# Opening of a fused attention and gated MLP block: left-over weight rows on ScalarE's queue and in pieces, column sums 32 wide, keys ahead, V of chunk 1 behind the transposes of chunk 2

## Chip, cores and metric

The kernel runs on one core of one Trainium2 chip. The metric is the device time of one execution in microseconds (us), lower is better. An engine is named as in the profile: PE is TensorE, DVE is VectorE, ACT is ScalarE, POOL is GpSimd, and SP is SyncE, which in this kernel only issues DMAs.

## The reference, cut to what matters

All inputs are bfloat16. S = 2048 tokens, D = 576, H = 32 heads of 18, F = 4608.

```python
mod = (silu(c) @ w_mod).reshape(1, 6, 1, 576)          # c is 1 x 576, w_mod is 576 x 3456
sa, ca, ga, sb, cb, gb = mod[:, 0], ..., mod[:, 5]
h = layernorm(x) * (1 + ca) + sa
x = x + ga * attention(h, wqkv, wo)                    # each token sees 8 keys: itself and 2, 4, ... 14 before it
h = layernorm(x) * (1 + cb) + sb
x = x + gb * (((h @ w_gate) * (h @ w_up)) @ w_down)
```

The reference's attention gathers eight keys and values for each token (missing ones at the start are masked), takes the softmax over the eight logits of each head, sums the values, and multiplies with wo.

## The kernel before

**Tiles.** The tokens are cut into eight chunks of 256 (CH), each of two tiles of 128 (ST). D = 576 is four full blocks of 128 rows and one left-over block of 64 rows. So every weight with 576 input rows has five k-tiles (KT), the last of which (kt = KF = 4) fills 64 partitions only; its other 64 partitions are set to zero.

**Order.** The schedule is manual: every engine runs its instructions in the order in which the program emits them. The order in the opening is written out by hand, as calls that interleave three chunks. Waits for data, and for buffers, are semaphores set by the tile framework from what is read and written. The DMAs that SP and ACT issue share eight semaphore slots, taken in turn in program order, and an issue waits for the landing of the DMA that held its slot before.

**Opening loads.** SP loads, in this order: x of chunk 0 in two tiles, the five k-tiles of wmA (the columns sa and ca of w_mod, order MODK), wqk (the query and key columns of wqkv, order QKK) with x of chunk 1 before the fourth, wv, x of chunk 2, wmB (sb, cb), wo in four pieces, wmC (ga), later tokens, wgr, and five blocks of gate and up weights (load_wgu). wgr holds the 64 left-over rows of w_gate and w_up, one above the other on 128 partitions, for all 4608 columns. ACT loads only c.

**Modulation columns.** `sc` is silu(c) as a column for each k-tile. `pm_part(kt)` multiplies the wmA blocks with it, ten matmuls for each kt, each of one output column; `pm` is the sum over kt. `run_idle(n)` puts n matmuls on zeros between. `t0(j)` transposes the normalised tile j of chunk 0, and `mod0` evicts it with the modulation into hT0. `qk0(j, kt)` accumulates queries and keys of tile j over k-tiles as they land; the calls go (0,0) (0,1) (1,0) (0,2) (1,1) (0,3) (1,2) (0,4) (1,3) (1,4), where the second number counts along QKK.

**Chunk 0's attention** is done without a gather: `pj` multiplies queries with shifted keys, `lj` sums them into logits, `max_j` and `sum_j` do the softmax, whose result is `attn`. `to_keys(j)` shifts `attn` from queries to keys by matmuls with a shifted identity (`slide`) into `pk`, and ACT copies that to `keyed`. `av_mul(j, hf)` multiplies the values with `keyed` on DVE, and `av_sum(j, hf)` sums the products, shifted, on TensorE into `po`.

**Chunks 1 and 2 beside it.** `a_t(i, ...)` transposes the normalised chunk i, tile by tile, and evicts five tiles of hT (three on DVE, two on ACT); `between` is called after the first token tile's transposes. hT comes from a pool with one buffer (`hTp`), so that chunk 2's hT lies where chunk 1's lay. `a_v(i, j)` computes the values of one token tile from hT and wv (matmuls `pv` and `pvr`), ACT copies them to `v_sb`, and a DMA on POOL's queue stores them. `a_q(i, g)` computes group g of queries and keys. `mod_columns` and `mod_row` make the other modulation values; the row of ga is two matmul groups, `pa` of 512 columns and `pb` of 64. `b_wj` ends chunk 0's attention with wo, `norm2` and `transposed` prepare h2T, and the matmuls of gate and up (L645) then run over groups of token tiles to the end of the kernel.

The part of the order that the change moves:

```python
    for j in range(ST):
        a_v(1, j)
    ga_out = []
    a_t(2, (0, 1, 2), lambda: ga_out.append(mod_row(..., ga_bc, sc_bc)))
    for j in range(ST):
        to_keys(j)
    ga_out[0]()
    av_mul(0, 0)
    av_mul(0, 1)
    a_q(2, 0)
    av_sum(0, 0)
```

Of the kernel before, what the change touches and what calls it, by code (L numbers as in the profile page):

```python
# [7 lines left out]
BF = mybir.dt.bfloat16  # L8
F32 = mybir.dt.float32
ALU = mybir.AluOpType  # L10
# [6 lines left out]
SYNC = mybir.DependencyInfo(mybir.DependencyClass.Sync, mybir.DependencyReason.DATA)  # L17

P = 128
D = 576  # L20
DP = 640
KT = 5
KF = 4
# [4 lines left out]
FF = 4608  # L28
# [5 lines left out]
ST = CH // P  # L34
# [2 lines left out]
VA = 28  # L37
VR = H - VA

MODK = (0, 1, 4, 2, 3)  # L40
QKK = (0, 1, 4, 2, 3)
GROUPS = [(0, 2), (2, 6), (6, 10), (10, 13), (13, 16)]

# [2 lines left out]
def kernel(  # L46
# [13 lines left out]
    nc = tc.nc  # L60
# [30 lines left out]
    def ps(shape, dt, name):  # L91
        return psp.tile(shape, dt, name=name, tag="bank")
# [4 lines left out]
    def col(m):  # L97
        return js(m) if m < KF else slice(D - P, D)
# [3 lines left out]
    addc = consts.tile([P, 2, KT], F32, name="addc")  # L102
    eps = consts.tile([P, 1], F32, name="eps")
    modc = consts.tile([P, 4, KT], F32, name="modc")
# [39 lines left out]
    def load_wgu(g):  # L144
        if g >= NG * NBLK:
            return
        cs = slice((g % NBLK) * NB, (g % NBLK + 1) * NB)
        wb = (wgx if g in (3, 4, NBLK - 1) else wgup).tile([P, KF, 2, NB], BF, name="wgu")
        for t, wsrc in enumerate((B_w_gate, B_w_up)):
            r = nc.sync.dma_start(wb[:, :, t, :], wsrc[0:KF * P, cs].rearrange("(k p) n -> p k n", p=P))  # L150
        wgu_blk[g] = wb
        wgu_in[g] = r

    def load_wgr():
        for t, wsrc in enumerate((B_w_gate, B_w_up)):
            r = nc.sync.dma_start(wgr[64 * t:64 * (t + 1), :], wsrc[KF * P:D, :])
        return r

    def load_wd(g):
        if g >= NG * NBLK:  # L160
# [6 lines left out]
    def load_k(dst, wsrc, c0, n):  # L167
        r = nc.sync.dma_start(dst(slice(0, P), slice(0, KF)), wsrc[0:KF * P, c0:c0 + n].rearrange("(k p) n -> p k n", p=P))
        nc.sync.dma_start(dst(slice(0, 64), KF), wsrc[KF * P:D, c0:c0 + n])
        return r  # L170

    def load_wm2(wm, blk):
        for p, k in ((slice(0, P), slice(0, KF)), (slice(0, 64), KF)):
# [10 lines left out]
    def run_idle(n):  # L184
        idle = ps([P, P], F32, "idle")
        for _ in range(n):
            nc.tensor.matmul(idle[:], lhsT=zero[:], rhs=zero[:], start=True, stop=True, skip_group_check=True)
# [5 lines left out]
    nc.vector.memset(addc[:, 1, :], 1.0)  # L193
    nc.scalar.dma_start(c_row[0:KF, :], c[0, 0:KF * P].rearrange("(m p) -> m p", p=P))
    nc.scalar.dma_start(c_row[KF:KT, 0:D - KF * P], c[0:1, KF * P:D])
    nc.scalar.preload_act_table_set("natural_log_exp_and_others")
    nc.gpsimd.memset(ident[:], 0.0)
    nc.gpsimd.affine_select(out=ident[:], in_=ident[:], compare_op=ALU.not_equal, fill=1.0, base=0,
                            pattern=[[-1, P]], channel_multiplier=1)
# [1 line left out]
    wmC = wdp.tile([P, FB, D], BF, name="wd")  # L201
    wmCr = x1p.tile([P, D], BF, name="x1")
    nc.gpsimd.memset(wmA[64:, KF, :, :], 0.0)
    nc.gpsimd.memset(wmCr[64:, :], 0.0)
    halves = lambda t: t.rearrange("p (b n) -> p b n", b=2)

    def rows(kt):
        return slice(0, P if kt < KF else 64), slice(kt * P, min(D, (kt + 1) * P))

    for kt in MODK:  # L210
        p, r = rows(kt)
        nc.sync.dma_start(wmA[p, kt, :, :].rearrange("p b n -> p (b n)"), w_mod[r, 0:2 * D])
    for kt in QKK:
        if kt == QKK[3]:
            load_x(1)
        p, r = rows(kt)
        nc.sync.dma_start(wqk[p, kt, :], A_wqkv[r, 0:2 * D])
    load_k(lambda p, k: wv[p, k, :], A_wqkv, 2 * D, D)


# [86 lines left out]
    def mod_row(wm, dst, sc_bc, parts=((0, 512), (512, D))):  # L307
        outs = []
        for c0, c1 in parts:
            p_t = ps([P, c1 - c0], F32, "pa" if c0 == 0 else "pb")  # L310
            for kt in range(KT):
                nc.tensor.matmul(p_t[:], lhsT=sc_bc[:, kt, :], rhs=wm(slice(0, P), kt)[:, c0:c1],
                                 start=(kt == 0), stop=(kt == KT - 1))
            outs.append((dst[:, c0:c1], p_t))

        def evict():
            for d, p_t in outs:
                nc.scalar.copy(d, p_t[:])
        return evict
# [15 lines left out]
    def a_tiles(i):  # L335
        hT = hTp.tile([P, KT, CH], BF, name="hT") if i else vshp.tile([P, KT, CH], BF, name="vsh")
        aa[i].update(hT=hT, qT=qTs[i % 2], kT=kTs[i % 2])
# [8 lines left out]
    def a_t(i, on_dve=(0, 1, 2), between=None):  # L346
        a_tiles(i)
        hT = aa[i]["hT"]
        transposed(aa[i]["xn"], lambda m: hT[:, m, :], (0, 1), 0, between)(on_dve)
# [25 lines left out]
    def a_q(i, g):  # L375
        qk_tiles(i, QGRP[g], slice(0, CH), nc.scalar.copy)
        if g == 2:
            a_halo(i)
# [4 lines left out]
    def a_v(i, j):  # L383
        hT = aa[i]["hT"]
        pv = ps([P, VA * DH], F32, "pv")
        pvr = ps([P, VR * DH], F32, "pvr")
        for kt in range(KT):
            nc.tensor.matmul(pv[:], lhsT=hT[:, kt, js(j)], rhs=wv[:, kt, 0:VA * DH], start=(kt == 0), stop=(kt == KT - 1))  # L388
        for kt in range(KT):
            nc.tensor.matmul(pvr[:], lhsT=hT[:, kt, js(j)], rhs=wv[:, kt, VA * DH:D], start=(kt == 0), stop=(kt == KT - 1))  # L390
        v_sb = vstage.tile([P, DH, H], BF, name="v_sb")[:] if i else v0(j)
        nc.scalar.copy(v_sb[:, :, 0:VA], pv[:].rearrange("p (h d) -> p d h", d=DH))
        nc.scalar.copy(v_sb[:, :, VA:H], pvr[:].rearrange("p (h d) -> p d h", d=DH))
        r0 = HALO + i * CH + j * P
        if i == 0:
            if j == 1:
                nc.gpsimd.dma_start(vd[r0 + P - HALO:r0 + P, :], o_sbs[0][P - HALO:P, j, 0:D])
            return
        nc.gpsimd.dma_start(vd[r0:r0 + P, :], v_sb.rearrange("p d h -> p (d h)"))
# [99 lines left out]
    def to_keys(j):  # L499
        pk = ps([P, W, H], F32, "pk")  # L500
        for w in range(W):
            sh = DIL * (W - 1 - w)
            at = attn0[:, w // 4, :, w % 4, :]
            cross = j == 0 and sh > 0
            nc.tensor.matmul(pk[:, w, :], lhsT=slide[:, P + sh:2 * P + sh], rhs=at[:, j, :], start=True, stop=not cross,
                             skip_group_check=True)
            if cross:
                nc.tensor.matmul(pk[:, w, :], lhsT=slide[:, sh:P + sh], rhs=at[:, 1, :], start=False, stop=True,
                                 skip_group_check=True)
        kt = lgp.tile([P, W, H], BF, name="keyed", tag="lgs")  # L510
        nc.scalar.copy(kt[:], pk[:])
        keyed.append(kt)
# [266 lines left out]
    c_col = ps([P, KT], F32, "c_col")  # L779
    nc.tensor.matmul(c_col[:], lhsT=c_row[:], rhs=ident[0:KT, 0:KT], start=True, stop=True)  # L780
    e_f = sp.tile([P, KT], F32, name="e_f")
    nc.scalar.activation(e_f[:], c_col[:], ACTF.Exp, scale=-1.0)
    stat0(0)
    rsq0(slice(0, 1))
    nc.vector.tensor_scalar_add(e_f[:], e_f[:], 1.0)
    nc.vector.reciprocal(e_f[:], e_f[:])
    nc.vector.tensor_tensor(sc[:], c_col[:], e_f[:], ALU.mult)
    stat0(1)
    rsq0(slice(1, 2))
    for j in range(ST):  # L790
        norm0(j)
    a_tiles(0)
    a_halo(0)
    nc.vector.memset(wo[64:, KF, :], 0.0)
# [6 lines left out]
    for kt in QKK:  # L801
        nc.gpsimd.tensor_copy(halves(wq4[:, kt, :]), halves(wqk[:, kt, :])[:, :, KF * P:D])

    pm = ps([P, 2, KT], F32, "pm")
    trA, trB = ps([P, 3, CH], BF, "tr_pA"), ps([P, 2, CH], BF, "tr_pB")
    tr = [trA[:, m, :] if m < 3 else trB[:, m - 3, :] for m in range(KT)]

    def pm_part(kt):
        for bi in range(2):
            for m in range(KT):  # L810
                nc.tensor.matmul(pm[:, bi, m:m + 1], lhsT=wmA[:, kt, bi, col(m)], rhs=sc[:, kt:kt + 1],
                                 start=(kt == MODK[0] and bi == 0 and m == 0), stop=(kt == MODK[-1]), skip_group_check=True)

    def t0(j):
        for m in range(KT):
            nc.tensor.transpose(tr[m][:, js(j)], xn0[:, j, js(m)], ident[:])

    run_idle(10)
    pm_part(MODK[0])
    run_idle(6)  # L820
    pm_part(MODK[1])
    t0(0)
    run_idle(4)
    t0(1)
    pm_part(MODK[2])
    run_idle(4)
    pm_part(MODK[3])
    run_idle(8)
    pm_part(MODK[4])
# [2 lines left out]
    def mod0(j, m, on_dve):  # L832
        modulate(hT0[:, m, js(j)], tr[m][:, js(j)], m, 1, 0, on_dve)

    nc.vector.tensor_tensor(modc[:, 0:2, 0:KF], pm[:, :, 0:KF], addc[:, :, 0:KF], ALU.add)
    mod0(0, 0, True)
    nc.vector.tensor_tensor(modc[0:64, 0:2, KF:KT], pm[64:P, :, KF:KT], addc[64:P, :, KF:KT], ALU.add)
    for j in range(ST):
        for m in (1, 2) if j == 0 else (0, 1, 2):
            mod0(j, m, True)  # L840
# [63 lines left out]
        nc.vector.tensor_tensor(attn0[:, :, j], dd0[:, j].rearrange("p (a w) h -> p a w h", a=2),  # L904
                                ss[:, None, None, :].to_broadcast([P, 2, 4, H]), ALU.mult)

    def behind(dma, load):
        tc.add_manual_dep(dma.ins, load.ins.name, SYNC, reason="value rows go first")

    load_x(2)  # L910
    wmB = sp.tile([P, KT, 2, D], BF, name="wmB", tag="wm")
    nc.gpsimd.memset(wmB[64:, KF, :, :], 0.0)
# [5 lines left out]
    load_k(lambda p, k: wmCr[p, :] if k == KF else wmC[p, k, :], w_mod, 2 * D, D)  # L918
    load_res(0)
    load_x(3)  # L920
    load_wgr()
    for g in range(5):
        load_wgu(g)

    for w in range(3):
# [38 lines left out]
    aa[2]["norm"]((0,))  # L964
    sum_j(1)
    aa[2]["norm"]((1,))
    for j in range(ST):
        a_v(1, j)
    ga_out = []
    a_t(2, (0, 1, 2), lambda: ga_out.append(mod_row(lambda p, k: wmC[p, k, :] if k < KF else wmCr[p, :], ga_bc, sc_bc)))  # L970
    for j in range(ST):
        to_keys(j)
    ga_out[0]()
    av_mul(0, 0)
    av_mul(0, 1)
    a_q(2, 0)
    av_sum(0, 0)
    av_mul(1, 0)
    av_sum(0, 1)
# [43 lines left out]
    first = []  # L1023
# [56 lines left out]
```

## Time and profile before

| quantity | value |
|---|---|
| median of 3 runs | 561.76 us (560.91 to 562.95) |
| profiled execution | 562.59 us |
| its span, first to last instruction | 560.9 us |
| busy PE / DVE / ACT / POOL | 550.2 / 330.7 / 248.5 / 67.1 us |
| moved by DMA | 108.14 MB, mean 193 GB/s |
| first matmuls of the opening | 1.06 us |
| first query and key matmul of chunk 0 | 11.78 us |
| first matmul of gate and up | 51.76 us |

The profiled execution is longer than its span by 1.69 us, which lie ahead of the first and behind the last instruction. "Busy" counts every recorded instruction, the matmuls on zeros too. In the timelines that follow a row is a group of like instructions on one engine: start and length in us, engine, line, operation, output and inputs, shape, count, and in brackets the idle time just before it with the engine or DMA that released it. Ends of matmuls are modelled, so that rows of PE can overlap. In the table by windows each engine's column is its busy time with the number of instructions in brackets, and the last three are the granted TensorE clock, the busy share of the DMA engines and what they moved.

### The profile page before, as it was taken

How to read it: one execution, taken by the hardware profiler on the slowest of the kernel's cores; microseconds unless marked ns; L12 is line 12 of the kernel's file. 1: busy time of each engine (PE TensorE's matmuls, PEld its weight loads, DVE VectorE, ACT ScalarE, POOL GpSimd, SP SyncE). 2: the span in 40 equal slices, each digit the busy share in tenths (PEclk: the TensorE clock that was granted, in tenths of full speed). 3: DMA queues.
4: the chain of work that ended last, by engine and by line, in shares of the span. 5: the costliest groups of instructions: out<-in, count | busy, mean ns of one | idle time of the engine just before them, and what ended most of it. 6: DMA issues, size and time to landing. Idle time of an engine off the chain costs nothing.

```text
span 560.9 us, 14310 instructions
## 1 busy us (share of the span) xinstructions
PE 550.2 (98%) x6019; PEld 329.5 (59%) x6057; DVE 330.7 (59%) x798; ACT 248.5 (44%) x572; POOL 67.1 (12%) x104
## 2 busy tenths in 40 slices
PE   8999999999999999999999999999999999999996
PEld 7878886665444446666444445655556555556564
DVE  6888898985677777251858686406736614322202
ACT  2645566344555662323355654230466511455500
POOL 5102201223000001111100100121100022000020
PEclk9999999999999999999999999999999999999999
DMA  8999999745646745232834856334966565565063
GB/s 252 279 270 307 341 295 352 238 131 172 239 153 200 241 149 177 70 125 96 292 122 151 266 174 190 85 106 128 326 184 196 182 196 174 183 191 187 1 172 115
DMA packets 69514, 108.14 MB, mean 193 GB/s; under 512 B 3562, under 2 KB 57658, under 8 KB 69322
## 3 DMA queue, kind: packets, MB, share of 16 engines
q1 hardware_dynamic: 58272, 61.42, 35.9%
q0 software_dynamic: 11168, 45.81, 25.6%
q8 instruction: 47, 0.77, 0.6%
q14 instruction: 17, 0.14, 0.1%
q10 hardware_dynamic: 10, 0.00, 0.0%
HBM read 102.78 MB, written 4.44 MB: 191 GB/s over the span
## 4 chain that ended last, share of the span: by engine, by line
PE 56%; issue 29%; POOL 3%; DMA 1%; DVE 1%; ACT 1%; POOLq 0%; ACTq 0%
PE pg L645 17%; PE pu L645 14%; PE acc L712 11%; PE pq L365 4%; POOL wd L165 2%; PE accr L716 2%; PE pw L562 2%; PE pv L388 2%; PE lg L423 1%; DMA wd<-in_B_w_down_dram 1%; PE tr_pA L287 1%; PE tr_pB L287 0%; PE oT_pA L493 0%; DVE o_t L751 0%; PE pwr L560 0%
## 5 line engine op out<-in xcount | busy, mean ns | idle before, releaser
L645 PE MATMUL pg<-h2T,wgu 64*128 64x512 bf16 (+2 forms) x1440 | 277.3, 334 | 0.0
L645 PE MATMUL pu<-h2T,wgu 64*128 64x512 bf16 (+2 forms) x1440 | 276.0, 334 | 0.0
L645 PEld LDWEIGHTS <-wgu 64*128 64x128 bf16 x2880 | 141.6, 94 | 106.9 <-issue 0.5
L669 ACT CAST u_sb<-pu 128x512 bf16<-128x512 f32 (+2 forms) x180 | 90.2, 501 | 136.1 <-PE pg L645 134.5
L712 PE MATMUL acc<-wd,hh 128*128 128x512 bf16 (+1 forms) x556 | 140.4, 370 | 0.4
L674 DVE TENSOR_TENSOR hh<-g_sb,u_sb 128x512 bf16<-128x512 bf16 (+2 forms) x180 | 66.7, 372 | 99.2 <-ACT g_sb L670 97.7
L716 PE MATMUL accr<-wd,hh 128*128 128x64 bf16 x576 | 99.4, 193 | 1.8 <-DMA wd<-in_B_w_down_dram 0.2
L670 ACT CAST g_sb<-pg 128x512 bf16<-128x512 f32 (+2 forms) x180 | 91.3, 507 | 0.0
L712 PEld LDWEIGHTS <-hh 128*128 128x128 bf16 x588 | 55.2, 98 | 57.8 <-issue 1.7
L165 POOL DMA_DIRECT2D wd<-in_B_w_down_dram x45 | 33.8, 751 | 292.3 <-PE accr L716 237.8
L645 PE MATMUL pu<-h2T,wgr 64*128 64x512 bf16 (+2 forms) x180 | 60.3, 335 | 0.3 <-ACT u_sb L669 0.3
L645 PE MATMUL pg<-h2T,wgr 64*128 64x512 bf16 (+2 forms) x180 | 60.3, 335 | 0.2 <-DVE h2T L274 0.2
L716 PEld LDWEIGHTS <-hh 128*128 128x128 bf16 x576 | 51.9, 98 | 3.2 <-issue 0.7
L413 DVE TENSOR_TENSOR prod<-qT,kT 128x1280 bf16<-128x1280 bf16 x56 | 44.8, 818 | 2.6 <-PE lg L423 2.6
L473 DVE TENSOR_TENSOR vsh<-vsh,attn 128x1152 bf16<-128x1152 bf16 x56 | 41.0, 751 | 0.0
L365 PE MATMUL pq<-hT,wqk 128*128 128x256 bf16 x280 | 35.3, 273 | 0.1
L274 DVE TENSOR_SCALAR h2T<-tr_pA,modc 128x256 bf16<-128x256 bf16 (+1 forms) x27 | 8.8, 382 | 36.9 <-PE tr_pA L287 36.9
L365 PEld LDWEIGHTS <-wqk 128*128 128x128 bf16 x280 | 25.6, 98 | 5.2 <-issue 0.4
L645 PEld LDWEIGHTS <-wgr 64*128 64x128 bf16 x360 | 18.0, 94 | 17.0 <-issue 4.5
L407 POOL DMA_DIRECT2D vsh<-vd x14 | 12.4, 890 | 123.3 <-DVE o_sb L484 84.4
L368 ACT CAST qT<-pq 128x512 bf16<-128x512 f32 x14 | 8.2, 582 | 27.8 <-PE pq L365 27.8
L480 DVE TENSOR_TENSOR vsh<-vsh 128x1152 bf16<-128x1152 bf16 x28 | 20.5, 752 | 0.0
(186 smaller groups left out, 485.5 us busy)
## 6 DMA issues: line engine op xcount, KB each, us to landing
wd<-in_B_w_down_dram POOLq DMA_DIRECT2D x45, 576.0 KB, 4.5
wgu<-in_B_w_gate_dram SPq DMA_DIRECT2D x45, 512.0 KB, 4.4
wgu<-in_B_w_up_dram SPq DMA_DIRECT2D x45, 512.0 KB, 5.6
vsh<-vd POOLq DMA_DIRECT2D x14, 1152.0 KB, 8.0
x_r<-in_A_x_dram SPq DMA_DIRECT2D x8, 288.0 KB, 7.4
out_dram<-x SPq DMA_DIRECT2D x15, 144.0 KB, 6.8
x_t<-in_A_x_dram SPq DMA_DIRECT2D x7, 288.0 KB, 5.7
vd<-v_sb POOLq DMA_DIRECT2D x14, 144.0 KB, 4.1
```

The costliest lines, as they stand in the source:

```text
L165: return nc.gpsimd.dma_start(wb[:], B_w_down[r0:r0 + FB * P, :].rearrange("(k p) n -> p k n", p=P))
L365: nc.tensor.matmul(pq[:, gi, :], lhsT=qk_w(kt, m), rhs=hT[:, kt, cols], start=(kt == 0), stop=(kt == KT - 1))
L407: return nc.gpsimd.dma_start(vsh[:].rearrange("p w d h -> p w (d h)"), vsrc)
L413: nc.vector.tensor_tensor(prod[:], aa[i]["qT"][:], aa[i]["kT"][:, :, off:off + CH], ALU.mult)
L473: nc.vector.tensor_tensor(v, v, at, ALU.mult)
L480: nc.vector.tensor_tensor(vsh[:, d], vsh[:, d], vsh[:, 4 + 2 * s:6 + 2 * s], ALU.add)
L645: return nc.tensor.matmul(bank[:, 0:N], lhsT=lhs, rhs=rhs, start=first, stop=last, skip_group_check=True)
L669: nc.scalar.copy(u[:, 0:N], pu[:, 0:N])
L670: nc.scalar.copy(g[:, 0:N], pg[:, 0:N])
L674: nc.vector.tensor_tensor(hh[:, f, 0:N], gu[0][:, 0:N], gu[1][:, 0:N], ALU.mult)
L712: nc.tensor.matmul(a[:], lhsT=hh[:, f, js(j)], rhs=wb[:, f % FB, cs], start=(f == 0), stop=(f == FT - 1))
L716: nc.tensor.matmul(accr[:, j, :], lhsT=hh[:, f, js(j)], rhs=wb[:, f % FB, 512:D], start=(f == 0 and j == 0), stop=(f == FT - 1), skip_grou ...
```

## The change

The left-over 64 rows (kt = 4) of wmA and of wqk are now loaded by ACT's queue: wmA's directly behind c, ahead of the load of the activation table, and wqk's after the second `rsq0`, with a dependency (`behind`) on the landing of wmA's k-tile 2. SP loads the full k-tiles 0 to 3 of both. MODK becomes (0, 4, 1, 2, 3). wgr is loaded in four quarters of its columns, each before the wgu block of the same number, eight DMAs in place of two.

`sc` is computed 32 columns wide (`sc_w`), and the matmuls of `pm_part` have 32 equal columns, of which the first is read. `sc` itself is copied from it behind the norms. The matmuls on zeros are put at other places: 20, 4, 2, 8 and 5 in place of 10, 6, 4, 4, 8 and 5 after the first 24.

Behind the softmax the order becomes: a_v(1,0), the ga row's first 512 columns, the transposes of chunk 2's first tile, the ga row's last 64 columns, `to_keys` of both tiles, the transposes of the second tile, a_v(1,1), then av_mul and a_q(2,0), and only then the evictions of the ga row.

```diff
-MODK = (0, 1, 4, 2, 3)
+MODK = (0, 4, 1, 2, 3)
...
-    def load_wgr():
+    def load_wgr(q):
+        cs = slice(q * FF // 4, (q + 1) * FF // 4)
         for t, wsrc in enumerate((B_w_gate, B_w_up)):
-            r = nc.sync.dma_start(wgr[64 * t:64 * (t + 1), :], wsrc[KF * P:D, :])
-        return r
+            nc.sync.dma_start(wgr[64 * t:64 * (t + 1), cs], wsrc[KF * P:D, cs])
...
-    nc.scalar.preload_act_table_set("natural_log_exp_and_others")
...
+    nc.scalar.dma_start(wmA[0:64, KF, :, :].rearrange("p b n -> p (b n)"), w_mod[KF * P:D, 0:2 * D])
+    nc.scalar.preload_act_table_set("natural_log_exp_and_others")
...
-    for kt in MODK:
+    def load_wmA(eng, kt):
         p, r = rows(kt)
-        nc.sync.dma_start(wmA[p, kt, :, :].rearrange("p b n -> p (b n)"), w_mod[r, 0:2 * D])
-    for kt in QKK:
-        if kt == QKK[3]:
+        return eng.dma_start(wmA[p, kt, :, :].rearrange("p b n -> p (b n)"), w_mod[r, 0:2 * D])
+
+    def load_qk(eng, kt):
+        p, r = rows(kt)
+        return eng.dma_start(wqk[p, kt, :], A_wqkv[r, 0:2 * D])
+
+    wmA_in = [load_wmA(nc.sync, kt) for kt in range(KF)]
+    for kt in range(KF):
+        if kt == 2:
             load_x(1)
-        p, r = rows(kt)
-        nc.sync.dma_start(wqk[p, kt, :], A_wqkv[r, 0:2 * D])
+        load_qk(nc.sync, kt)
...
-    nc.vector.tensor_tensor(sc[:], c_col[:], e_f[:], ALU.mult)
+    wide = lambda t: t[:, :, None].to_broadcast([P, KT, 32])
+    nc.vector.tensor_tensor(sc_w[:], wide(c_col), wide(e_f), ALU.mult)
     stat0(1)
     rsq0(slice(1, 2))
+    behind(load_qk(nc.scalar, KF), wmA_in[2])
     for j in range(ST):
         norm0(j)
+    nc.vector.tensor_copy(sc[:], sc_w[:, :, 0])
...
-    pm = ps([P, 2, KT], F32, "pm")
+    pm = ps([P, 2, KT, 32], F32, "pm")
...
-                nc.tensor.matmul(pm[:, bi, m:m + 1], lhsT=wmA[:, kt, bi, col(m)], rhs=sc[:, kt:kt + 1],
+                nc.tensor.matmul(pm[:, bi, m, :], lhsT=wmA[:, kt, bi, col(m)], rhs=sc_w[:, kt, :],
...
-    run_idle(10)
+    run_idle(20)
     pm_part(MODK[0])
-    run_idle(6)
     pm_part(MODK[1])
     t0(0)
     run_idle(4)
+    pm_part(MODK[2])
     t0(1)
-    pm_part(MODK[2])
-    run_idle(4)
+    run_idle(2)
     pm_part(MODK[3])
     run_idle(8)
     pm_part(MODK[4])
...
-    load_wgr()
     for g in range(5):
+        if g < 4:
+            load_wgr(g)
         load_wgu(g)
...
-    for j in range(ST):
-        a_v(1, j)
-    ga_out = []
-    a_t(2, (0, 1, 2), lambda: ga_out.append(mod_row(lambda p, k: wmC[p, k, :] if k < KF else wmCr[p, :], ga_bc, sc_bc)))
-    for j in range(ST):
-        to_keys(j)
-    ga_out[0]()
+    a_v(1, 0)
+    ga_row = lambda part: mod_row(lambda p, k: wmC[p, k, :] if k < KF else wmCr[p, :], ga_bc, sc_bc, (part,))
+    ga_out = [ga_row((0, 512))]
+
+    def between():
+        ga_out.append(ga_row((512, D)))
+        for j in range(ST):
+            to_keys(j)
+
+    a_t(2, (0, 1, 2), between)
+    a_v(1, 1)
     av_mul(0, 0)
     av_mul(0, 1)
     a_q(2, 0)
+    for out in ga_out:
+        out()
     av_sum(0, 0)
```

The reads of `pm` take column 0 of the 32, and `behind` moves to an earlier place in the file with its text unchanged.

## The prediction

> **What bounds the kernel now.** I read the page first, sections 1 and 4, then TensorE's waits, then stage windows and timelines of the opening, the only stage the diff reaches.
>
> ```profile
> PE 550.2 (98%) x6019; PEld 329.5 (59%) x6057; DVE 330.7 (59%) x798; ACT 248.5 (44%) x572; POOL 67.1 (12%) x104
> ```
>
> TensorE is busy for 550.2 of 560.9 us. The matmuls of gate_up begin at 51.76 (first h2T wait) and are dense from there, so what the opening gains or loses before 51.76 I pass on to the end one for one. The waits of TensorE up to 60 us say how little there is:
>
> ```profile
> PE idle L187 <- DVE c_row L190: 1.1, 1, 1.1
> PE pm L811 <- DMA wmA<-in_w_mod_dram: 0.9, 2, 0.6
> PE po L531 <- DVE vsh L520: 0.7, 1, 0.7
> PE lgj L888 <- DVE prodj L880: 0.3, 1, 0.3
> ```
>
> But "busy" counts idle matmuls (L187) that only keep the array warm; in the first 17 us they hide waits for loads. The windows show that stage (engine columns: busy, count; last three: clock, DMA share, GB/s):
>
> ```profile
> 3.50:7.00 3.50, 2.69 (x30) 1.94 (x28) 3.27 (x10) 1.07 (x5) 3.23 (x10) 1.00 0.92 257
> 7.00:10.40 3.40, 3.35 (x55) 3.35 (x56) 1.85 (x9) 0.07 (x1) 1.46 (x4) 1.00 1.03 336
> 10.40:13.20 2.80, 2.63 (x33) 2.39 (x32) 2.01 (x9) 1.25 (x4) 0.88 (x3) 1.00 1.07 307
> 13.20:17.00 3.80, 3.80 (x69) 3.69 (x67) 2.44 (x8) 0.70 (x4) 1.31 (x3) 1.00 1.08 343
> 25.00:29.00 4.00, 4.00 (x80) 3.71 (x79) 3.90 (x12) 2.38 (x6) 0.00 (x0) 1.00 1.14 294
> ```
>
> The DMA engines are full from 3.5 on. By the DMA issues of the trace wqk2 lands at 14.91 and wqk3 at 15.88, and the first matmuls that need them start at 14.96 and 15.97: the last two loads of the query and key weights set the end of that stage. From 17.6 DVE (3.97 of 4, 3.90 of 4) and PE are both full until 33. The second place is there: chunk 0 needs `keyed` and chunk 2 its hT (timelines: start, length, idle before):
>
> ```profile
> 31.12 1.23 PE L388 MATMUL pv<-wv,hT 128*128 128x504 bf16 x5
> 33.85 0.33 PE L287 MATMUL tr_pA<-ident,ln_xn 128*128 128x128 bf16 x3
> 34.71 1.64 PE L365 MATMUL pq<-hT,wqk 128*128 128x256 bf16 x10
> 37.06 1.10 PE L531 MATMUL po<-slide,vsh 128*128 128x142 bf16 x15 [0.71 <-DVE vsh L520]
> ```
> ```profile
> 32.68 0.42 DVE L904 TENSOR_TENSOR attn<-dd,ssj 128x256 bf16<-128x256 f32 x1
> 34.22 1.04 DVE L274 TENSOR_SCALAR hT<-tr_pA,modc 128x256 bf16<-128x256 bf16 x3 [0.56 <-PE tr_pA L287]
> 35.65 2.63 DVE L520 TENSOR_TENSOR vsh<-o_sb,keyed 128x2304 bf16<-128x2304 bf16 x2 [0.38 <-ACT keyed L511]
> ```
>
> DVE stands idle 0.56 for the second transpose and 0.38 for `keyed`, and TensorE then 0.71 for the first weighted values.
>
> **Part 1, column sums 32 wide.** Column copies go from 128x1 to 128x32: fifty matmuls. Ten pm of one column take 0.29 us to the next row (5.67 to 5.96); the 128x32 matmuls at L505 follow each other by 0.025 us, so the price is nearly the same. Below 13.19 matmuls of 128 columns start 0.107 us apart, above it 0.056: the array runs at half speed until 13.19 (the clock column reads 1.00 throughout, so the spacing is what I use). One-column matmuls leave the array mostly empty. Adding up columns streamed, I get 62%, 60% and 79% use in the three 3.41 us stretches ending at 13.19; with 32 columns and twenty idle matmuls ahead, the first would be about 95%, so I expect the change of spacing near 6.4. What it shortens ((0,0) and (0,1) of qk0 by 0.35 us each, the first stages by the pm waits 0.57 and 0.29) is hidden by wqk2 and wqk3: worth 0, and up to 0.25 if cover were gone. The wide product on DVE (128x160) replaces one of 128x5; I charge 0.1 beside the load waits, plus a copy after the norms: 0. The order "kt 4 second" follows the new loads: 0.
>
> **Part 2, kt 4 of both weights on ScalarE's queue.** SP has two issues less (0.43 us each, ahead of work that waits for landing, not issue: 0). wmA4 now starts at the front, wqk4 after wmA2 has landed (8.28), with ACT waiting for that. Behind it on ACT are the mod0 evictions, not wanted before pm is done at about 9.8: no cost. The bytes ahead of wqk3 are the same. The 64-row pieces keep the stream about 0.6 us longer than their bytes deserve (first engine 0.93 to 1.0 us for 144 KB, against 0.75 for 288 KB). Bounds: if both overlap with others, 1.2 us come out, plus 0.2 for the clock; if the extra queue only mixes packets, wqk3 lands 0.3 later. I take 0.2 faster, near the bottom, because the DMA share is already at 1.0 in the rows.
>
> The Trainium skill, "DMA: Bandwidth & Descriptors", section "Issuing engines are not separate DMA queues", says that transfers from another engine run on the same 16 DMA engines and save only the issue time; its rules add that two halves by partition serialize. By that this part is worth 0 and the sum would be 0.2 higher. The rows so far agree with it (share at 1.0), but 257 GB/s beside 343 leaves room.
>
> **Part 3, keys ahead and V behind T.** Matmuls are the same, in another order. The hT pool has one buffer. a_v(1,1) reads chunk 1's hT, and now it stands behind chunk 2's transposes, so the five hT evictions of chunk 2 (DVE three, ACT two) must wait for its last pvr matmul. Queued behind: on DVE av_mul, on ACT v_sb and qT; for av_mul waits po. The working: attn ends at 32.68+0.42=33.10. The keys' matmuls take 0.58 (34.13 to 34.71): 33.70. The second transposes 0.28: 33.98. a_v(1,1) 1.22 (31.12 to 32.34): 35.20, and 0.2 until its last result is through: 35.40. hT on DVE 1.04: 36.44, where av_mul begins (before 35.65; `keyed` was ready long ago). po follows 1.41 after av_mul's start (37.06-35.65): 37.85, against 37.06: 0.8 later. The ends are +0.3 (evictions and the matmul's tail overlap as much as rows of 0.33 permit, and PE finds other work) and +1.1. I take +0.8, as each step has its own row. What else moves has cover: v_sb(1,1) on ACT comes 3 us later and its store on POOL with it, read back only for chunk 1's values, after gate_up has begun; the ga row's first part now comes at 31.1 and needs wmC, which lands at 29.54 (1.6 of cover; without it, that much on PE); ga_bc is evicted behind qT, and first used by x at 41.5 on DVE. All 0. TensorE's idle time in 33 to 38 would rise from 0.84 (5.00-4.16) to about 1.6 to 1.9.
>
> **Part 4, wgr in eight pieces.** Six more issues on SP at 0.43 are 2.6 us, where SP waits for landings anyway. wgr landed at 36.29 and 38.91, wgu0 at 42.2, the use is at 51.76: 9 us of cover. If that were gone it would cost the excess over it. wgu5 waits for a buffer that TensorE frees (issue 56.46) and lands 1.45 before use, moving with TensorE. 0.
>
> **Sum.** -0.2 + 0.8 = +0.6 against the profiled execution: 562.59 + 0.6 = 563.2. That execution took 0.83 more than the median of the runs (561.76), so the median comes to 562.4. Its own range, -0.6 to +1.4, is 561.2 to 563.2. Less than 0.3% (1.7 us) is about what a measurement of this kernel can tell from no change.
>
> **Rivals.** (B) The second queue fills the stream. Speaking for it: only 257 GB/s at 3.5 to 7 and 307 at 10.4 to 13.2, with 343 to 401 in the half-microsecond slices from 12 to 15. The 3.8 MB between 3.5 and 15.9 (the four rows' sum) would take 10.6 instead of 12.4: 1.8 earlier, and 0.8 of the half-row waste: 2.6 earlier. PE could follow, as pm and eight qk0 of 0.5 us need no more than 4 us from 9.2. Net -2.6+0.8=-1.8: 560.0. Against: share 1.0. Chance 0.28.
> (C) The hT wait is hidden: then the gain of the keys stands, DVE's idle 0.38 goes, av_mul begins at 35.15 and po at 36.55: -0.5-0.2=-0.7, 561.1. Against: one buffer. Chance 0.08.
> (D) The clock falls back to half speed. With a warm array from 6.4 the same matmuls use half of it, about 30% between 6.4 and 13.2, below the 60% that did not warm it before. If a stretch with so little use takes the clock away, the stretch from 13.2 to 16.6, or the next, runs at 0.107 again. There PE holds six qk0 groups of 0.5 us at present; half of a stretch's 3.4 us is lost, 1.7, less 0.2 that load waits cover: +1.5. Net -0.2+0.8+1.5=+2.1: 563.9. It decides when PE's use in one stretch falls under a limit that this trace doesn't show. Chance 0.22, into which I put small mishaps of the queues.
> By the Trainium skill, "TensorE: Matmul & The Clock Gate", Part 1, the window is 3413 ns and the clock goes back only after an idle window; no window here is idle, so (D) would give nothing and the time would be that of the forecast. The trace has the rise at 13.19 and none of its falls before the end.
> (A) The forecast: 0.42.
>
> So faster by over 0.3% is B, 0.28; slower by over 0.3% is D, 0.22; within is A and C, 0.50. The range 559.6 to 564.2 reaches from B to D with some tenths for the scatter of runs; outside lie B with its full bounds and D over two stretches.
>
> **What would show it.** Spacing 0.056 from about 6.4 (part 1). wqk3 landing and (0,4) starting near 15.7: A; near 13.3: B. hT on DVE not starting before 35.2, released by PE pvr, and av_mul near 36.2 to 36.4: A; hT at 34 and no idle: C. Spacing 0.107 again after 13: D. Gate_up starting at 52.4 and the end moved alike. I am wrong if the start of gate_up moves by more than 1.7 either way, or if the time moves without it.

## The result and the profile after

The changed kernel takes 564.51 us (median of 20 runs, 563.03 to 566.16) against 561.80 for the kernel before (20 runs): the ratio is 1.0044, 95% interval 1.0030 to 1.0059. It is slower, by about 2.5 us, and lies outside the predicted range. The profiled execution has a span of 562.9 us (before: 560.9).

The waits of TensorE up to 60 us show a new first line, and as another new one the last, where a group of chunk 2's queries and keys waits for hT:

```profile
PE pq L866 <- DMA wqk<-in_A_wqkv_dram: 2.7, 1, 2.7
PE idle L190 <- DVE c_row L193: 1.1, 1, 1.1
PE tr_pA L829 <- DVE ln_xn L267: 0.8, 1, 0.8
PE pm L824 <- DVE sc_w L798: 0.5, 1, 0.5
PE pq L374 <- DVE hT L283: 0.5, 1, 0.5
```

The 2.7 us stand ahead of (0,2), the third group of qk0's tile 0 and the fourth in order. The timeline of TensorE there (start, length, idle before):

```profile
11.23 0.61 PE L866 MATMUL pq<-vsh,wqk 128*128 128x128 bf16 x8
11.67 0.22 PE L866 MATMUL pq<-vsh,wq 128*128 128x128 bf16 x1
14.56 1.04 PE L866 MATMUL pq<-vsh,wqk 128*128 128x128 bf16 x8 [2.67 <-DMA wqk<-in_A_wqkv_dram]
15.39 0.31 PE L866 MATMUL pq<-vsh,wq 128*128 128x128 bf16 x1
15.49 1.06 PE L866 MATMUL pq<-vsh,wqk 128*128 128x128 bf16 x8
```

In the kernel before, (1,0) and (0,2) follow each other without a wait. POOL there waits for the same k-tile 4 to copy from it, and the first tile's groups end in DVE's kT copy:

```profile
13.44 0.61 PE L854 MATMUL pq<-vsh,wqk 128*128 128x128 bf16 x8
13.94 0.61 PE L854 MATMUL pq<-vsh,wqk 128*128 128x128 bf16 x8
12.46 0.29 POOL L802 COPY wq<-wqk 128x128 bf16<-128x128 bf16 x1 [0.28 <-DMA wqk<-in_A_wqkv_dram]
16.40 0.69 DVE L860 CAST kT<-pq 128x512 bf16<-128x512 f32 x1 [1.29 <-PE pq L854]
```

Two things are to be seen. After (1,0) the array of the changed kernel stands still until wqk's k-tile 4, the third in QKK, lands at 14.51; in the kernel before it landed at about 12.41, 0.05 ahead of POOL's copy. K-tile 2 had been there since 13.35. And the groups that follow take 0.93 us (14.56 to 15.49) where the one before the wait took 0.50: the clock is at half. The stretches show it in the column after POOL's:

```profile
10.85:14.27 3.42, 1.04 (x19) 0.87 (x16) 2.63 (x10) 1.04 (x3) 0.00 (x0) 1.00 1.07 296
14.27:17.68 3.41, 3.12 (x30) 3.13 (x31) 0.00 (x0) 0.00 (x0) 1.82 (x4) 0.51 1.07 361
```

The granted clock falls for one stretch of 3.41 us after a stretch in which TensorE was busy for 1.04. DVE then waits for qk0, and, 19 us later, for V of chunk 1:

```profile
18.50 0.69 DVE L872 CAST kT<-pq 128x512 bf16<-128x512 f32 x1 [4.95 <-PE pq L866]
...
37.41 1.05 DVE L283 TENSOR_SCALAR hT<-tr_pA,modc 128x256 bf16<-128x256 bf16 x3 [1.76 <-PE pvr L399]
38.38 3.88 DVE L529 TENSOR_TENSOR vsh<-o_sb,keyed 128x2304 bf16<-128x2304 bf16 x3
```

DVE's kT copy, the end of qk0's first tile, moves from 16.40 to 18.50 (+2.10), and po from 37.06 to 39.78 (+2.72, of which 0.62 arise between the two). The first gate and up matmul moves from 51.76 to 54.47 (+2.71), and the span by 2.0; 0.35 of the difference are two short waits for wd (0.11 and 0.24, after 470) that the profile before has and this one lacks.

A half-clock stretch lowers the mean granted clock of a 561 us span by 0.5 x 3.41/561 = 0.003, so an execution with a mean of 0.997 or less most likely had one (a fall in the last two us of the span takes 0.001 to 0.002). The half speed of the first microseconds does not enter this mean: the column reads 1.00 there, and the profile before, at half speed until 13.19 by its spacing, has a mean of 0.999. Of the 20 executions of the changed kernel, 15 have a mean of 0.997 or less (median 564.7) and five have more (563.4).

### The profile page after: what moved, and what is told of

The parts are those of the page before. It is cut to its first block, busy times and chain, and to the rows that moved or that the text cites. A ratio compares the mean times of both kernels' runs of the same rounds, so it can differ in the third digit from the quotient of the medians.

```text
span 562.9 us, 14324 instructions
## 1 busy us (share of the span) xinstructions
PE 548.8 (97%) x6021; PEld 328.1 (58%) x6059; DVE 330.7 (59%) x799; ACT 248.4 (44%) x572; POOL 66.8 (12%) x104
## 4 chain that ended last, share of the span: by engine, by line
PE 88%; DVE 1%; issue 1%; ACT 1%; ACTq 0%
PE pg L654 28%; PE pu L654 22%; PE acc L721 20%; PE pq L374 4%; PE accr L725 4%; PE pw L571 3%; PE pv L397 2%; PE lg L432 2%; PE tr_pA L296 1%; PE oT_pA L502 1%; PE tr_pB L296 1%; PE pwr L569 0%; DVE o_t L760 0%; PE lt L448 0%; PE pvr L399 0%
```

## The experiments

From here on: theory L says that three things in the opening make the loss, namely the late k-tile 4, the clock's fall that its wait brings, and V behind the transposes. Rival C says that a warm array falls back whatever waits there are. Rival W puts the loss on wgr in pieces. Two distances serve as measures: the start of DVE's kT copy (end of the load stage), and from there to the start of po (the order behind the softmax). "Half clock" counts executions with a mean clock of 0.997 or less, that is, with a fall after the first rise.

| kernel | ratio to before (95%) | median us | half clock | kT copy | po after it |
|---|---|---|---|---|---|
| changed | 1.0044 (1.0030 to 1.0059) | 564.51 | 15 of 20 | 18.50 | 21.28 |
| e1 k-tile 4 on SP | 0.9987 (0.9968 to 1.0007) | 561.53 | 1 of 12 | 15.15 | 21.42 |
| e2 filler matmuls | 1.0021 (0.9999 to 1.0043) | 563.93 | 0 of 12 | 16.98 | 21.28 |
| e3 old order behind softmax | 1.0022 (0.9996 to 1.0047) | 563.72 | 5 of 12 | 16.69 | 20.57 |
| e4 k-tile 4 fourth | 0.9999 (0.9979 to 1.0020) | 562.43 | 0 of 12 | 16.17 | 21.30 |
| e15 k-tile 4 early on ACT | 0.9979 (0.9962 to 0.9997) | 561.63 | 0 of 12 | 14.78 | 21.41 |
| e5 new order alone | 1.0003 (0.9981 to 1.0024) | 562.59 | 6 of 12 | 15.22 | 21.94 |
| e9 wide columns alone | 0.9975 (0.9955 to 0.9995) | 561.04 | 0 of 12 | 15.02 | 20.70 |
| e10 wmA's rows on ACT alone | 1.0014 (0.9989 to 1.0039) | 562.87 | 5 of 12 | 15.25 | 20.57 |
| e11 wgr in pieces alone | 0.9979 (0.9956 to 1.0002) | 562.92 | 7 of 12 | 15.96 | 20.56 |
| e13 all but wqk's rows and the order | 0.9959 (0.9935 to 0.9984) | 560.99 | 0 of 12 | 15.16 | 20.70 |
| e8 k-tile 4 on SP, V first | 0.9969 (0.9949 to 0.9990) | 561.11 | 0 of 12 | 15.31 | 20.81 |
| e12 wide, keys between | 0.9942 (0.9919 to 0.9965) | 560.27 | 0 of 12 | 15.22 | 20.01 |

The kernels ran in several groups, each against the kernel before on its own chip (its medians there: 561.90 for e1 to e4, 562.22 for e5, e8, e9 and e10, 562.87 for e11 to e13, 562.09 for e15), so ratios are compared rather than times. (A ratio can differ a little from the quotient of the two medians.)

**e1: k-tile 4 back on SP.**

```diff
-    for kt in range(KF):
-        if kt == 2:
+    for kt in QKK:
+        if kt == QKK[3]:
             load_x(1)
         load_qk(nc.sync, kt)
...
-    behind(load_qk(nc.scalar, KF), wmA_in[2])
```

> The changed kernel with wqk's left-over rows issued by SP again, in third place as before; wmA's stay on ACT. Theory L (the changed kernel loses 0.6 us because wqk's k-tile 4 lands at 14.51 instead of 12.41 while it is the third that qk0 needs, 1.0 to 1.5 us more because the array, idle 2.7 us, falls back to half clock, and 0.7 us because V of chunk 1 stands between the transposes of chunk 2 and their eviction): k-tile 4 lands near 12, no idle time over 1 us before qk0's third group, spacing 0.056 throughout from 6.4 at the latest, DVE's kT copy at 16.4 or a little before, po still 0.7 later than that: time 0.3 to 0.8 us above before. Rival C (the fall comes from the array being warm early, so that any load wait takes the clock): spacing 0.107 again after 13, time 1.5 to 2.0 us above before. Rival W (the loss is wgr in pieces and other loads after 24 us): as the changed kernel, 2.5 above before.

The 2.7 us wait is gone (two of 0.4 and less remain), the clock stays at full, and the loss is gone too, where +0.3 to +0.8 had been expected. The kT copy, at 15.15, is even earlier than theory L had it: 16.40 in the profile before was no good measure of that kernel, as e14 shows below. C and W fall here: the array is at full clock from 4.9 on and wgr is in pieces in this kernel too.

**e2: matmuls on zeros in place of the wait.**

```diff
     for j, i in ((0, 0), (0, 1), (1, 0), (0, 2), (1, 1), (0, 3), (1, 2), (0, 4)):
+        if (j, i) == (0, 2):
+            for _ in range(44):
+                nc.tensor.matmul(pqk[0][2][:], lhsT=zero[:], rhs=zero[:], start=False, stop=False, ...)
         qk0(j, QKK[i])
```

> The changed kernel with 44 matmuls on zeros (about 2.45 us at 0.056) added into qk0's third group, just ahead of the late k-tile 4: the array stays used while it waits. Theory L: the load still lands at 14.5, the clock stays at full, qk0's third group starts at 14.56 and the last of tile 0 ends near 17.0 instead of 18.4; DVE's kT copy at 17.1; time 0.9 to 1.5 below the changed kernel, 1.0 to 1.6 above before. Rival C: clock falls all the same, time as the changed kernel. Rival W: as the changed kernel too, with the kT copy earlier and the gain not reaching gate_up.

The load is as late as ever (14.17), but the groups behind it run at 0.50 us:

```profile
12.09 2.62 PE L880 MATMUL pq<-zero 128*128 128x128 bf16 x44
14.54 0.61 PE L866 MATMUL pq<-vsh,wqk 128*128 128x128 bf16 x8
14.99 0.22 PE L866 MATMUL pq<-vsh,wq 128*128 128x128 bf16 x1
15.05 0.61 PE L866 MATMUL pq<-vsh,wqk 128*128 128x128 bf16 x8
```

The kT copy comes at 16.98, 1.52 before that of the changed kernel: that is about the clock's price in an execution that falls. Two other figures bound it. The profile of e3 below has the same opening and happened not to fall, with a kT copy at 16.69, 1.81 earlier; and the changed kernel's own executions differ by 1.3 us in the median (564.7 with a fall, 563.4 without). The median of e2 is only 0.6 us below that of the changed kernel, less than the expected 0.9 to 1.5: a quarter of the executions of the changed kernel does not fall, and the 44 matmuls hold the group back until 14.54, 0.37 after the landing. The rest, 15.2 to 17.0, is the order: five groups of 0.5 us have to run after the late load, instead of one or two.

**e3: the old order behind the softmax** (that part of the diff undone).

> The changed kernel with the order behind the softmax as it was before (both a_v of chunk 1 first, keys and the ga row's evictions behind the transposes). Theory L: qk0 as in the changed kernel (idle 2.7, half clock), but po starts 2.0 later than before instead of 2.7: time 0.7 below the changed kernel, 1.8 above before. Rival (the order costs nothing or gains, and all the loss is in the loads): time as the changed kernel or above it.

po stands 20.57 after the kT copy, as in the kernel before (20.66), and not 21.28. The median fell by 0.8 us; the intervals of the two ratios overlap, and fewer executions fell to half clock (5 of 12, against 15 of 20), so that the time alone would not show it.

**e4: the late tile taken fourth.**

```diff
-QKK = (0, 1, 4, 2, 3)
+QKK = (0, 1, 2, 4, 3)
```

> The changed kernel with QKK = (0, 1, 2, 4, 3): qk0 takes k-tile 2 third and k-tile 4 fourth, in the order in which they land (13.35, 14.51, 14.82). Theory L: idle time ahead of qk0's third group 1.6 instead of 2.7, the last group of tile 0 starts near 15.5 and DVE's kT copy near 16.1, 0.3 before that of the kernel before; the clock stays at full in most runs: time 0.2 to 0.7 above before, with V's 0.7 left in it. Rival C: the clock falls again, kT copy near 17.5, time 1.5 above before. Rival W: no more than 0.5 below the changed kernel.

K-tile 4 landed at 14.69, as late as ever, and yet the kernel is level with the one before: with two groups moved ahead of it the wait is 1.43, no execution falls to half clock, and three groups instead of five stand behind it.

**e15: the same queue, an earlier issue.** Whether the rows were late because of ACT's queue or because they were issued late (8.06, behind wmA's k-tile 2) was still open.

```diff
     wmA_in = [load_wmA(nc.sync, kt) for kt in range(KF)]
+    load_qk(nc.scalar, KF)
...
-    behind(load_qk(nc.scalar, KF), wmA_in[2])
```

> The changed kernel with wqk's left-over rows still on ACT's queue, but issued early (about 3.9, behind the table load) and not behind wmA's k-tile 2 (8.06). The order behind the softmax is the changed one. If the late issue made k-tile 4 late: it lands before wqk's k-tile 1, near 9 to 10.5, qk0's third group doesn't wait for it, no half-clock stretch after 13, kT copy at 15.1 to 15.5, time as with the rows on SP in third place (0.4 below before to 0.3 above). Rival (rows on ACT's queue land late because two queues share the engines): landing near 14 again and time 1.5 or more above before.

Issued at 3.01, between wmA's k-tiles 2 and 3, the rows land at 9.04, and qk0 does not wait for them at all:

```profile
11.60 0.61 PE L866 MATMUL pq<-vsh,wqk 128*128 128x128 bf16 x8
12.04 0.22 PE L866 MATMUL pq<-vsh,wq 128*128 128x128 bf16 x1
12.10 0.61 PE L866 MATMUL pq<-vsh,wqk 128*128 128x128 bf16 x8
```

The queue was harmless, the time of issue was not. The Trainium skill says in "DMA: Bandwidth & Descriptors", section "Issuing engines are not separate DMA queues", that transfers run on the same 16 engines, whichever engine starts them, and interleave. The traces agree: from issue to landing the rows took 6.0 and 6.5 us on ACT's queue (e15, changed) and about 7.1 on SP's (before, 5.30 to 12.41), and in the changed kernel ACT's k-tile 4, issued at 8.06, landed before SP's k-tile 3, issued at 5.89 (14.51 and 14.82).

**e5: the new order alone, on the kernel before.**

> The kernel before with the new order behind the softmax alone (ga row ahead, keys between the two transposes, V of the second tile behind them). Theory L: the hT evictions of chunk 2 wait for PE's last pvr of a_v(1,1); relative to DVE's kT copy of qk0, po starts 0.7 to 0.8 later than in the kernel before; time 0.5 to 0.8 above before. Rival (the order is neutral or gains, and the late po in the changed kernel came from loads or the clock): po at the old distance or closer, time 0 to 0.6 below before.

In the trace po comes 21.94 after the kT copy, 1.3 later than before; 0.4 of that is a gap between pvr matmuls to which the trace gives no releaser, and its cause stays open. The time, +0.4 us, is not distinguishable from none. That the order costs rests on the distances: 20.56 to 20.70 in all kernels with the old order in the table, 21.28 to 21.42 in those with the new one on the changed kernel.

**e9, e10, e11: one part each on the kernel before.** The wide columns with their matmuls on zeros (e9), wmA's left-over rows on ACT (e10), wgr in pieces (e11).

> The kernel before with the column sums 32 wide and the new places of the matmuls on zeros alone; all loads and the order behind the softmax as before. Theory L: clock at full from about 6.4 at the latest, but qk0 waits for the same landings: kT copy at 16.3 to 16.5, time within 0.3 of before, and no gain from the clock alone. Rival (the clock and not the loads made the gain of the first experiment, kT copy at 15.2): kT copy at 15.3 to 15.7, time 0.7 to 1.1 below before.

> The kernel before with only the 64 left-over rows of wmA on ACT's queue (MODK 0, 4, 1, 2, 3); columns narrow. Theory L, load side: wqk's k-tile 3 lands near 14.7 instead of 15.88, as in the first experiment, while the array is still at half clock until about 13; kT copy at 15.2 to 15.8, time 0.5 to 1.2 below before. Rival (the landing of k-tile 3 moved for another reason than this load, or varies by a microsecond from run to run): landing near 15.9, kT copy at 16.4, time within 0.3 of before.

> The kernel before with only wgr loaded in eight pieces, each pair ahead of the wgu block of its number. Theory L: nothing before 24 us changes, the loads from 25 to 54 land some 1 to 2 us earlier or later without being waited for; time within 0.3 of before. Rival W (the pieces cost): 0.5 or more above before, with a wait for wgu or wgr in the gate and up matmuls.

e9 is a miss for theory L: the wide columns alone make the kernel faster, ratio 0.9975. A part of the reason is the last column but two of the table. Kernels with narrow columns have a half-clock stretch in 6, 5 and 7 of 12 executions, and the kernel before itself in 56 of 116, where its median is 563.6 instead of 561.9; the seven kernels with wide columns in which no late tile is taken third have one in 84. It is not the whole reason: in the group of e9 the executions of the kernel before without such a stretch have a median of 561.93, and e9 has 561.04. The late first rise is a candidate for the rest (13.19 in the profile before, 3.8 in that of e9), but no run shows it. Whether the columns or the matmuls on zeros that came with them do it was not separated.

e10's opening came out as theory L had it (k-tile 3 landed at 14.58, kT copy at 15.25), but the time did not follow: no gain, where 0.5 to 1.2 us were expected. e14, which follows, shows why this proves nothing of the load: the kernel before has such openings too. e10 and e11 are within their intervals of no change.

**e14: the kernel before, profiled again.**

> The kernel before, unchanged, for a second profile of its opening. If the first one (wqk's k-tile 3 landing at 15.88, kT copy at 16.40, half clock until 13.19) was an unlucky execution: landing at 14.5 to 14.9, kT copy at 15.1 to 15.4. If it is the rule: 15.7 to 16.0 and 16.3 to 16.5.

```profile
15.54 0.69 DVE L860 CAST kT<-pq 128x512 bf16<-128x512 f32 x1 [0.22 <-PE pq L854]
```

Two stretches of the same profile, all engines:

```profile
6.40:9.80 3.40, 3.01 (x54) 3.01 (x55) 2.45 (x11) 0.50 (x2) 1.99 (x5) 0.64 0.98 313
9.80:13.20 3.40, 3.11 (x52) 2.79 (x51) 2.03 (x8) 1.50 (x4) 0.88 (x3) 0.86 1.06 303
```

K-tile 3 lands at 14.99 and not 15.88. The clock, in the column after POOL's, had risen early and fell for a stretch (7.33 to 10.74), and yet this execution took 561.22 us, less than the median of those without a fall: at that place the waits for loads most likely hid it. With e5 and e11, which have the same opening (14.70 and 15.09), the kT copy of the kernel before lies at 15.22 to 15.96, and the profile on which the prediction was built was the latest of four. Against their mean of 15.8 the changed kernel lost 2.7 us up to there in its profile, which has a fall.

**e8 and e13: parts of the change kept.** e13 is e1 with the old order behind the softmax; e8 is e1 with a_v(1,1) ahead of the transposes:

```diff
     a_v(1, 0)
+    a_v(1, 1)
...
     a_t(2, (0, 1, 2), between)
-    a_v(1, 1)
```

> The changed kernel with wqk's left-over rows on SP again and the order behind the softmax as before: what is left of the change are the wide columns, wmA's left-over rows on ACT and wgr in pieces. Theory L: the two last add nothing to the wide columns: no half-clock stretch, kT copy at 15.0 to 15.3, time as the wide columns alone, 1.2 below before. Rival (they take away, by mixing rows of two queues, or wgr costs): 0.5 below before or worse.

> The changed kernel with two edits: wqk's left-over rows on SP again in third place, and a_v(1,1) ahead of chunk 2's transposes, with the keys still between them. Theory L: kT copy near 15.2 as in the first of these experiments, then hT on DVE released by the transposes and not by pvr, no wait for keyed, po 20.0 to 20.3 after the kT copy instead of 20.7 (before) and 21.4 (changed): po near 35.3; time 1.6 to 2.4 below before, 4 to 5 below the changed kernel. Rival (the earlier part's gain is given back to a later wait, as DVE and PE are full from 17 on and loads of wmB and wmC come no earlier): time 0.3 to 0.8 below before, with a new wait between 24 and 50.

e13 comes out as expected, level with e9 (560.99 and 561.04): what is left of the change, without the late tile and the new order, is faster than the kernel before. e8 missed: hT is released by the transposes, yet po comes 20.81 after the kT copy and not 20.0 to 20.3, and the time is 1.1 us below before and not 1.6 to 2.4.

```profile
33.75 1.05 DVE L283 TENSOR_SCALAR hT<-tr_pA,modc 128x256 bf16<-128x256 bf16 x3 [1.14 <-PE tr_pA L296]
```

Ahead of the second transposes now stand the ga row's 512 columns, its 64 and the keys; they begin at 33.38, and DVE waits 1.14 for them, where it waited 0.56 in the kernel before.

**e12: the keys between the transposes, the ga row behind them,** on e9.

```diff
-    ga_out = []
-    a_t(2, (0, 1, 2), lambda: ga_out.append(mod_row(..., ga_bc, sc_bc)))
-    for j in range(ST):
-        to_keys(j)
-    ga_out[0]()
+    def between():
+        for j in range(ST):
+            to_keys(j)
+
+    a_t(2, (0, 1, 2), between)
+    ga_out = mod_row(..., ga_bc, sc_bc)
     av_mul(0, 0)
     av_mul(0, 1)
     a_q(2, 0)
+    ga_out()
```

> The kernel of the experiment with the wide columns alone, and in it another order behind the softmax: both a_v of chunk 1, chunk 2's first transposes, the keys of both tiles, the second transposes, and the whole ga row only then. Theory L: the second transposes wait for the softmax and the keys (about 0.6) instead of the ga row (1.2), keyed is ready before av_mul, the ga row fills TensorE while DVE evicts hT: po 20.0 to 20.3 after the kT copy instead of 20.7, time 0.4 to 0.7 below the wide columns alone, 1.5 to 1.9 below before. Rival (TensorE is full there, so an order gains nothing): po at 20.7, time as the wide columns alone, 1.2 below before.

```profile
32.86 1.05 DVE L277 TENSOR_SCALAR hT<-tr_pA,modc 128x256 bf16<-128x256 bf16 x3 [0.42 <-PE tr_pA L290]
33.82 3.89 DVE L523 TENSOR_TENSOR vsh<-o_sb,keyed 128x2304 bf16<-128x2304 bf16 x3
```

The wait for keyed is gone, that for the transposes is 0.42, TensorE works on the ga row meanwhile and has no idle time ahead of po, which comes 20.01 after the kT copy. At 560.27 us, ratio 0.9942, this is faster than both kernels: by 2.6 us in the median than the one before in the same group, while the changed kernel, in its own, stands at 1.0044.

## Why the prediction was wrong, by its own steps

- **Part 2 failed, and this is the step.** It priced ACT's waiting for wmA's k-tile 2 by what is queued behind it on ACT, "no cost", and compared the bytes ahead of wqk3. It did not ask who waits for the moved load itself. QKK has k-tile 4 third, so that five groups stand behind it; it was issued at 8.06 instead of 5.30 and landed at 14.51 instead of 12.41. wqk3, whose landing the prediction took for the end of the stage, came at 14.82, and nobody waited for it. e1, e4 and e15 each take the loss away by another means. The term, -0.2 in the sum, measures +3.0 (changed kernel against e1, in the medians). With -1.2 for part 1 (e9), +0.7 for part 3 and 0 for part 4 the sum is +2.5, about the change that was measured.
- **Rival D had the clock's behaviour, but not what sets it off.** The clock does fall after a stretch with little use. D saw the cause in a warm array that needs half the time for the same matmuls; e1 and e15 are warm as early and fall in 1 of 24. What lowered the use was the wait of part 2, which the prediction did not know of. D put the use at about 30% from 6.4 on; in the three stretches from 4.08 it was 46, 73 and 24%. +1.5 was forecast, and 1.52 is the difference between e2 and the changed kernel in the trace; with 1.3 and 1.8 by the other two figures, and the price worked out for another stretch, a match this close is luck. The last of these is the stretch ahead of the fall, where the matmuls of 10.91 to 11.73 fill 0.82 of 3.41 us. In "TensorE: Matmul & The Clock Gate", Part 1, the Trainium skill has a window of 3413 ns, which the recorded half-clock stretch of 3.41 us matches, and lets the clock go back after an idle window. The "only" in the prediction's sentence on it is not the page's word. That stretch was not idle, and yet the clock fell; the measurement decides.
- **Part 3 was right.** +0.8 was worked out; the distance from kT copy to po grows by 0.6 to 0.8, and the line that was named, hT released by pvr with idle time of 1.76, is there. Rival C (the wait is hidden) falls. One sign of this part failed: TensorE's idle time was to rise from 0.84 to 1.6 or more, and in the same stretch, moved by the 2.10 of the load stage (35.10 to 40.10), it is 0.88.
- **Part 1 was mis-sized.** The rise came early, at 4.1 us and not near 6.4. "Worth 0, and up to 0.25 if cover were gone" should have been about -1.2 (e9, in the medians), in part because the kernel before loses the clock again in about half of its executions. The single profile had no such fall (mean 0.999), only a late rise, and so could not show them. The use before that rise, 62, 60 and 79%, comes out as 64, 63 and 84% if 0.107 us is counted for 128 columns; the reading stays the same.
- **The load term, -0.2, and rival B** cannot be told from scatter: the k-tile that lands last did so at 14.2 to 15.1 in the other kernels, old loads or new, and at 15.88 in the one profile of before. No run shows the second queue filling the stream.
- **Part 4 was right** within what e11 can show: 0, interval -0.44% to +0.02%.
- **That the opening passes on to the end one for one** held: 2.71 at the first gate and up matmul, 2.0 to 2.7 in span and medians.

## What to carry to other kernels

When a load moves to another queue or behind a wait, look first for its own consumer and count the work that is queued behind that consumer: here a 144 KB load held back five groups of an accumulation because it was taken third and landed fourth, 2.1 us later than before. A wait on TensorE can cost more than its length where little else keeps the array in use (here 2.7 us of wait, and 1.3 to 1.8 for the clock), so either take the operands in the order in which they land, or fill the gap. And where a stage hangs on load landings and the clock, one profile is one draw; look at the mean clock of all runs, and at a second profile, before a microsecond of it is used as a term.

## What the runs showed of the hardware that was not expected

- The granted clock fell for one stretch of 3.41 us behind a stretch with 24% of matmul use (in the profile; 15 of 20 executions have a mean clock that tells of a fall); with 44 matmuls on zeros in the gap it fell in none of 12.
- The 15 profiles put a limit on it. Counting 0.056 us for 128 columns, in steps of 3.41 us from the first rise, the falls in the opening came behind stretches with 24% (changed, 10.91 to 14.32), 36% (e14, 3.91 to 7.33) and 37% (e10, 5.00 to 8.41), and none came behind a stretch with 40% or more (e5, 5.16 to 8.57: 40%; e4's wait of 1.43: 53%). At the end of the kernels the limit shows again: a fall behind 38% (e1, from 554.42), none behind 38% (e4, from 555.62). So by this count it lies near 38%. It also means that the place of a wait in its stretch matters: in e3 the same late load cut across two stretches, 44% and 73%, and the clock stayed.
- By the same count the first stretch at full clock holds 36 to 40% in e5, e10 and e14, with narrow columns, and 41 to 47% in those with wide columns that rise as early, at 3.8 to 5.2 (changed, e1, e8, e9, e12 and e15); of these the wide columns make up 8 to 12 points, without which five of the six would lie below the limit. No run separates the columns from the matmuls on zeros.
- The kernel before had half-clock stretches in 56 of 116 executions, which were 1.8 us longer in the median (not each: e14 was not), with no change of program between them. With 32 equal columns for each weight block instead of one, and the matmuls on zeros that came with them, it was 1 of 84 in the kernels that take no late tile third.
- The same 64 rows landed 6.0 us after issue when issued at 3.01, and 6.5 us after when issued at 8.06 on the same queue: with the stream full, a load held back is late by about as much as it was held. The two queues are not one line, though: in the changed kernel the rows on ACT's queue overtook a k-tile that SP had issued 2.2 us earlier.
